# H3 and S5 sequence layers on one core: the halo rows of k are loaded unshifted and moved by one partition on TensorE, and the first loads change queues

## The chip, the core and the metric

The kernel runs on one core of a Trainium2 chip. The core has TensorE (PE, matrix products into PSUM), VectorE (DVE), ScalarE (ACT), GpSimd (POOL) and SyncE (SP); here SP only issues DMAs, and POOL issues some too. The metric is the device time of one execution in microseconds (us), lower is better.

## What is computed

Two layers with 2048 positions and 1024 channels stand side by side in the output. Layer A is an H3 layer: k is filtered over four neighbouring positions, multiplied by v, convolved with a long filter through an FFT of length 4096, and multiplied by q. Layer B is an S5 layer: a complex diagonal recurrence between two matrix products. Cut to what matters:

```python
# A: shift convolution with 4 taps, gate by v, long convolution, skip term, gate by q
k_pad = jnp.pad(k, ((0, 0), (3, 0), (0, 0)))
for t in range(4):
    k_shift = k_shift + k_pad[:, t:t + S, :] * shift_k[:, 3 - t][None, None, :]
kv = k_shift * v
y  = irfft(rfft(kv, 2 * S) * rfft(ssm_k, 2 * S))[:S]
a  = q * (y + kv * ssm_D)
# B: h[t] = Lam_bar * h[t-1] + Bu[t]
Bu = einsum("bld,pd->blp", x, B_bar)          # B_bar from Lambda, log_dt, B_re, B_im
y  = 2 * einsum("blp,dp->bld", hseq, C).real + x * Dskip
out = concat([a, b], axis=-1)                  # bfloat16
```

## The kernel before

**An order written out by hand.** The whole kernel is a list of tasks in a string, `ORDER` (L63 to L132). A word such as `wbe.6` calls the function `E["wbe"](6)`; `@S`, `@G` and `@D` choose SP, GpSimd or DVE for it; `:b9` and `:p0` name the SBUF or PSUM slots that it takes. Each engine runs its own instructions strictly in this order, so the place of a word decides what is queued behind it. DMAs go to SP by `spd` and to GpSimd by `gpd` unless the word says otherwise (L156, L157).

**The shift convolution of A (DVE).** Position 16n+s of k lies in partition n, row s. The tile `kring` holds 8 rows per partition; `kp.r` (L546) loads rows 2r and 2r+1 into slots (2r+4) mod 8. Position 16n needs the three positions before it, which lie in partition n-1. For them `kp.-2` and `kp.-1` load rows 12 to 15 into slots 0 to 3, one partition further down: partitions 1 to 127 take what belongs to 0 to 126, in two DMAs each (112 and 15 partitions). Partition 0 has no predecessor; a GpSimd memset (L370) fills its four slots with zeros. `kvm.r` (L561) multiplies the ring by the taps, `kva`, `kvb` and `kvc` add the products up and multiply by v.

**The taps.** `ld_w` (L376) loads `shift_k` as two rows into one partition; `wb.b` (L389) spreads 512 of its elements over all partitions by a matmul with a row of ones, and `wbe.b` (L394) copies the result from PSUM into `wbc`, all eight times. `kvm.0` needs all eight and the halo.

**The parameters of B.** `ld_par` (L237) loads four vectors into the 32 rows of `praw`; `par_T` transposes them on PE, `p32` copies them out on DVE, and `exp1`, `dve2`, `dve3`, `sm_pre`, `tabA1`, `exp2`, `sin0`, `tabA2`, `sin1`, `par_rest` and `sin2` make the constants and rotation tables from them on ACT and DVE.

**The matrix B.** `bl.j.w` loads a 128x1024 block of B_re or B_im, `bT.j.w` transposes it on PE (8 transposes into the PSUM slot p0 or p1), `bc.j.w` copies it into `BT` (L456). `bx` and `x` (L460, L466) are loads that transpose on the way, always on SP. `U.i.jp.jl` (L477) multiplies `BT` by x, `ue` evacuates, and `r1`, `r2`, `sc`, `r3`, `r4` run the recurrence on DVE.

**The transforms of A.** `hl` loads the long filter (`hk`), `hT` transposes it, `hc` evacuates on ACT, `am` and `hm` are the first DFT stage, `ae` and `he` evacuate it, `ast` and `hst` store it to DRAM for the later stages (L596 to L703).

Of the kernel before, what the change touches and what calls it, by code (L numbers as in the profile page):

```python
# [15 lines left out]
F32 = mybir.dt.float32  # L16
BF16 = mybir.dt.bfloat16
# [5 lines left out]
NR = 16  # L23
# [37 lines left out]
NX = 0  # L61

ORDER = """  # L63
bl.0.1:b0 bl.1.0:b11 bl.1.1@G:b14 ld_w@S:a0a11 bl.2.0@G:b13 ld_par bl.3.1@G:b12 bT.0.1:p0 bl.3.0:b10 bT.1.0:p1 kp.-2 kp.-1 bc.0.1 kp.0 ld_F@S par_T:p0
ld_sd@S:w0 p32 x.1:b9 bc.1.0@D wb.2:p0 exp1 wb.6:p1 wbe.6 dve2 wbe.2 dve3 wb.4:p1 sm_pre bl.0.0:b8 wb.3:p0 bx.5.1 wbe.4 wbe.3 wb.5:p1 tabA1:a10a9a8a7 wb.1:p0
wbe.1 wbe.5 bT.3.0:p0 exp2 tabA2 sin0 rt@G bT.3.1:p1 bx.7.0 sin1 par_rest kp.1 bc.3.1 bl.2.1:b7 x.0:b6 bc.3.0 wb.7:p1 wbe.7 bT.2.0:p0 vp.0:a5 wb.0:p1
bx.4.1 wbe.0 sin2 bT.0.0:p1 kvm.0:m0 bc.2.0 eo.1 bT.1.1:p0 hl.0:c0 eo.3 bx.7.1 bc.0.0 kva.0 bc.1.1 vp.2:a2 U.1.0.0:p1 bx.6.0 eo.0 bT.2.1:p0 eo.2 stt.1 U.1.0.1
bc.2.1 kvb.0:a6 z1 U.1.1.0:p0 stt.0 U.1.1.1 kvc.0 kvm.2:m0 am.0.1:d0 ue.1.1:a3 ue.1.0 hT.0.0:p0 kp.2 hT.0.3:p1 x.2:b0 hc.0.0:b5 ae.0.1:b4 hT.0.2:p0 am.1.0:d2
hc.0.2:b3 hm.0.0.0:d1 vp.1:a11 am.0.0:d0 ae.1.0:b2 bx.6.1 stt.3 he.0.0.0:b1 am.1.1:d2 kva.2 hT.0.1:p0 hc.0.3:b11 hm.0.0.1:d1 kp.3 hT.0.5:p1 bx.5.0 hc.0.5:b10
# [65 lines left out]
def full_kernel(ctx, tc, A_q, A_k, A_v, A_shift_k, A_ssm_k, A_ssm_D, B_x, B_Lre, B_Lim, B_Bre, B_Bim,  # L135
# [3 lines left out]
    nc = tc.nc  # L139
    P = 128  # L140
    S, D = A_q.shape[-2], A_q.shape[-1]
# [10 lines left out]
    q, k, v, x = A_q[0], A_k[0], A_v[0], B_x[0]  # L152
# [3 lines left out]
    spd = lambda o_, i_: (nc.gpsimd if on[0] == "G" else nc.sync).dma_start(o_, i_)  # L156
    gpd = lambda o_, i_: (nc.sync if on[0] == "S" else nc.gpsimd).dma_start(o_, i_)  # L157

    const = ctx.enter_context(tc.tile_pool(name="const", bufs=1))
# [3 lines left out]

    ident = const.tile([P, P], BF16, name="ident")
    make_identity(nc, ident[:])
    ones = const.tile([1, P], BF16, name="ones")
    nc.vector.memset(ones[:], 1.0)
    hpi = const.tile([P, 1], F32, name="hpi")
# [19 lines left out]
    kr = k.rearrange("(n s) d -> n s d", s=NR)  # L188
# [12 lines left out]
    st, pools, cms = {}, {}, {}  # L201

    def ap_pool(name):
        if name not in pools:
            for o in list(cms):
                cms.pop(o).__exit__(None, None, None)
            cms[name] = tc.tile_pool(name=name, bufs=1)
            pools[name] = cms[name].__enter__()
        return pools[name]
# [6 lines left out]
    def dtile(name):  # L216
        return psum.tile([P, 2, 512], F32, name=name, tag="pd%d" % cur["d"].pop(0), bufs=1)
# [12 lines left out]
    E = {}  # L230
# [135 lines left out]
    def kv_space():  # L366
        a1 = ap_pool("a1")
        st["wbc"] = a1.tile([P, 4, DV], BF16, name="wbc", bufs=1)
        st["kring"] = a1.tile([P, c["kr"], D], BF16, name="kring", bufs=1)
        nc.gpsimd.memset(st["kring"][0:1, 0:4, :].bitcast(F32), 0.0)  # L370
        if NX:
            st["kT"] = a1.tile([P, NX, NR + 4, P], BF16, name="kT", bufs=1)
            st["dg"] = a1.tile([P, NX, 4, P], BF16, name="dg", bufs=1)
# [74 lines left out]
    def copy(o_, i_):  # L448
        if on[0] == "D":
            nc.vector.tensor_copy(o_, i_)  # L450
        elif on[0] == "G":
            nc.gpsimd.tensor_copy(o_, i_)
        else:
            nc.scalar.copy(o_, i_)
# [90 lines left out]

    def kp(r):  # L546
        s0 = (2 * r + 4) % c["kr"]
        t_ = st["kring"][:, s0:s0 + 2, :]
        if r >= 0:
            spd(t_, kr[:, 2 * r:2 * r + 2, :])  # L550
        else:
            spd(t_[1:113, :, :], kr[0:112, NR + 2 * r:NR + 2 * r + 2, :])
            spd(t_[113:P, :, :], kr[112:P - 1, NR + 2 * r:NR + 2 * r + 2, :])
    E["kp"] = kp

    def vp(r):
        st["v", r] = k4("v", [P, 2, D])
        spd(st["v", r][:], vr[:, 2 * r:2 * r + 2, :])
# [197 lines left out]
@with_exitstack  # L756
def kernel(
    ctx: ExitStack,
    tc: tile.TileContext,
    A_q: bass.AP,  # L760
    A_k: bass.AP,
    A_v: bass.AP,
    A_shift_k: bass.AP,
    A_ssm_k: bass.AP,
    A_ssm_D: bass.AP,
    B_x: bass.AP,
    B_Lambda_re: bass.AP,
    B_Lambda_im: bass.AP,
    B_B_re: bass.AP,
    B_B_im: bass.AP,  # L770
    B_C_re: bass.AP,
    B_C_im: bass.AP,
    B_log_dt: bass.AP,
    B_Dskip: bass.AP,
    out: bass.AP,
):
    full_kernel(ctx, tc, A_q, A_k, A_v, A_shift_k, A_ssm_k, A_ssm_D, B_x, B_Lambda_re, B_Lambda_im,
                B_B_re, B_B_im, B_C_re, B_C_im, B_log_dt, B_Dskip, out)
# [30 lines left out]
```

## Time and profile before

| What | Value |
|---|---|
| median of 3 runs | 364.98 us (364.03 to 365.0) |
| profiled execution, its own time | 366.88 us |
| its span | 365.1 us, so 1.8 us lie around the span |
| granted TensorE clock, mean | 0.993 |
| first slices of 10 us, DMA share | 0.70, then 1.10, 1.25, 1.00 |
| POOL busy in the first 10 us | 4.51 us |

Times of the trace count from the start of the span. In a timeline, a row gives start, duration, engine, line, operation, output and input, and in brackets how long the engine sat idle before it and what ended that. "SPq" and "POOLq" are the queues' issue of DMAs. In a table by windows the columns are the stretch, its length, then busy time and instruction count of PE, PEld, DVE, ACT and POOL, the granted clock, the share of time that the DMA engines were busy, and GB/s.

### The profile page before, as it was taken

To read this page: it belongs to the slowest core of one execution; us is meant where nothing else is said; L and a number is where in the kernel's file an instruction comes from. 1 tells how busy PE (TensorE), PEld (TensorE's weight loads), DVE (VectorE), ACT (ScalarE), POOL (GpSimd) and SP (SyncE) were. 2 spreads that over 40 slices of the span, in tenths; PEclk is the share of its full clock that TensorE was granted. 3 is DMA by queue.
4 is the path that set the end of the run, shared out by engine and by line. 5 is a ranking of instruction groups with operands and counts; after the bars stand their busy time and mean duration, and the time that the engine had idled before them with its cause. 6 is when DMAs were issued, how large, how long until landed. Compare 5 with 4: busy or idle time off the path is not lost.

```text
span 365.1 us, 9551 instructions
## 1 busy us (share of the span) xinstructions
PE 336.0 (92%) x4109; PEld 215.8 (59%) x4109; DVE 319.3 (87%) x257; ACT 258.7 (71%) x330; POOL 65.4 (18%) x119
## 2 busy tenths in 40 slices
PE   4568898776999999999999999999999999999994
PEld 2366686664776986446475665654467568574441
DVE  3899999999999999999298999998998969989820
ACT  4799979558888976436477888887888784173641
POOL 4100111002014011300022313011041221344230
PEclk9999999998999999999999999999999999999999
DMA  6999998999998999888049977799986776989883
GB/s 205 275 333 308 251 406 307 213 343 248 265 287 281 204 225 307 263 228 203 0 111 303 212 275 233 235 227 355 282 239 226 203 257 193 348 254 316 293 246 116
DMA packets 74525, 91.95 MB, mean 252 GB/s; under 512 B 46369, under 2 KB 52401, under 8 KB 74482
## 3 DMA queue, kind: packets, MB, share of 16 engines
q1 hardware_dynamic: 64754, 58.55, 60.0%
q0 software_dynamic: 9728, 32.79, 27.1%
q8 instruction: 32, 0.52, 0.6%
q14 instruction: 11, 0.09, 0.1%
HBM read 47.28 MB, written 33.55 MB: 221 GB/s over the span
## 4 chain that ended last, share of the span: by engine, by line
PE 79%; ACT 7%; SPq 6%; DMA 5%; issue 2%; ACTq 0%
PE ps_y L532 31%; PE ps_u L477 28%; PE ps_a L664 5%; PE ps_a L694 4%; PE ps_a L630 3%; PE ps_a L596 3%; SPq L468 2%; DMA hk<-in_A_ssm_k_dram 2%; PE ps_a L725 2%; ACT ysb L601 2%; PE ps_y L537 2%; SPq L460 2%; ACT hT L622 2%; ACT ysbh L637 2%; DMA Ys_h<-ysbh 2%
## 5 line engine op out<-in xcount | busy, mean ns | idle before, releaser
L477 PEld LDWEIGHTS <-BT 128*128 128x128 bf16 x2048 | 119.5, 99 | 25.0 <-issue 13.2
L477 PE MATMUL ps_u<-xT,BT 128*128 128x128 bf16 x2048 | 126.8, 221 | 7.3 <-DMA xT<-in_B_x_dram 2.5
L532 PE MATMUL ps_y<-ct,h 128*128 128x512 bf16 x512 | 124.8, 380 | 0.0
L532 PEld LDWEIGHTS <-h 128*128 128x128 bf16 x512 | 44.3, 98 | 54.1 <-issue 12.5
L509 DVE TENSOR_TENSOR_SCAN h<-rtab,h 128x1040 bf16<-128x1040 f32 x32 | 72.5, 2307 | 0.1
L672 ACT CAST s<-ps_a 128x1024 bf16<-128x1024 f32 x64 | 62.0, 1016 | 12.7 <-PE ps_a L664 10.9
L542 ACT CAST yo<-ps_y 128x512 bf16<-128x512 f32 x32 | 18.9, 592 | 39.9 <-PE ps_y L532 32.6
L482 ACT CAST u<-ps_u 128x512 bf16<-128x512 f32 x64 | 37.9, 599 | 12.7 <-PE ps_u L477 12.6
L637 ACT CAST ysbh<-ps_a 128x1024 bf16<-128x1024 f32 x32 | 32.1, 1033 | 9.8 <-PE ps_a L630 8.4
L491 DVE TENSOR_TENSOR mt<-u,Z 128x4096 bf16<-128x4096 bf16 x16 | 36.6, 2285 | 2.8 <-ACT u L482 2.3
L569 DVE TENSOR_TENSOR mt<-kring,wbc 128x2048 bf16<-128x2048 bf16 (+3 forms) x14 | 35.7, 2588 | 1.6 <-DMA BT<-in_B_B_re_dram 1.6
L491 DVE TENSOR_TENSOR mt<-h,Z 128x4096 bf16<-128x4096 bf16 x16 | 36.6, 2289 | 0.2
L701 ACT CAST vsb<-ps_a 128x1024 bf16<-128x1024 f32 x32 | 30.9, 1015 | 7.2 <-PE ps_a L694 6.0
L601 ACT CAST ysb<-ps_a 128x1024 bf16<-128x1024 f32 x32 | 32.2, 1032 | 5.2 <-PE ps_y L537 1.5
L678 DVE TENSOR_TENSOR pq<-s,s 128x2048 bf16<-128x2048 bf16 x16 | 19.5, 1220 | 14.6 <-ACT s L672 14.4
L537 PE MATMUL ps_y<-Dd,xT 128*128 128x128 bf16 x128 | 28.0, 219 | 0.0
L157 POOL DMA_DIRECT2D Ys_kv<-ysb x14 | 7.8, 558 | 75.9 <-ACT ysb L601 75.9
L630 PE MATMUL ps_a<-hT,F1t 128*128 128x512 bf16 x64 | 19.3, 386 | 2.2 <-ACT hT L622 1.7
L596 PE MATMUL ps_a<-acc,F1t 128*128 128x512 bf16 x64 | 18.7, 384 | 2.3 <-ACT ysb L601 1.6
L682 DVE TENSOR_TENSOR s<-s,s 128x2048 bf16<-128x2048 bf16 x16 | 19.6, 1223 | 0.6
L503 DVE TENSOR_TENSOR h<-mt 128x2048 bf16<-128x2048 bf16 x16 | 19.6, 1224 | 0.4
L537 PEld LDWEIGHTS <-xT 128*128 128x128 bf16 x128 | 12.5, 98 | 12.3
(113 smaller groups left out, 326.6 us busy)
## 6 DMA issues: line engine op xcount, KB each, us to landing
Ys_h<-ysbh SPq DMA_DIRECT2D x23, 256.0 KB, 4.0
vv<-Vs POOLq DMA_DIRECT2D x11, 512.0 KB, 5.9
Ys_kv<-ysb SPq DMA_DIRECT2D x18, 256.0 KB, 4.2
Vs<-vsb SPq DMA_DIRECT2D x18, 256.0 KB, 3.5
kring<-in_A_k_dram SPq DMA_DIRECT2D x8, 512.0 KB, 4.3
v<-in_A_v_dram SPq DMA_DIRECT2D x8, 512.0 KB, 5.3
hk<-in_A_ssm_k_dram SPq DMA_DIRECT2D x8, 512.0 KB, 4.4
l2h<-Ys_h SPq DMA_DIRECT2D x8, 512.0 KB, 4.3
```

The source lines that it names most:

```text
L477: nc.tensor.matmul(pu[:, w, jl, :], BT[:, 2 * jp + jl, w, d, :], xT[:, d, :], start=(d == 0), stop=(d == ND - 1))
L482: nc.scalar.copy(u[:, :, 2 * jp:2 * jp + 2, :], st["pu", i, jp][:])
L491: nc.vector.tensor_mul(m, s_, w_)
L509: nc.vector.tensor_tensor_scan(gf, rtab[:].rearrange("p j t -> p (j t)"), gf, 0.0, ALU.mult, ALU.add)
L532: nc.tensor.matmul(py[:], h[:, 1 - w, j, 2:TP], st["CT", dh][:, j, w, :], start=(j == 0 and w == 0), stop=(j == NJ - 1 and w == 1))
L537: nc.tensor.matmul(py[:, dl * P:(dl + 1) * P], st["xT", i][:, d, :], Dd[:, d, :], start=False, stop=False)
L569: nc.vector.tensor_mul(m[:, :, j0:j0 + n, :], a_, wbc[:, j0:j0 + n, :].unsqueeze(1).to_broadcast([P, 2, n, DV]))
L601: nc.scalar.copy(st["ysb", r, u][:], st["pa", r, u][:].rearrange("p e d -> p (e d)"))
L630: nc.tensor.matmul(pd[:, e, :], F1t[:, u, :], st["hT", f, rp][:, e, :], start=True, stop=not sk)
L637: nc.scalar.copy(st["yh", f, rp, u][:], st["pa", f, rp, u][:])
L672: nc.scalar.copy(s16[:, u, :, :], st["ps", key, gq][u][:])
L701: nc.scalar.copy(vsb[:, gi, :].rearrange("p (e d) -> p e d", e=2), st["ps", "v", gq][gi][:])
```

## The change

The halo is loaded as it lies in DRAM, over all 128 partitions: row 13 into ring slot 0 and rows 14 and 15 into slots 6 and 7 (`kh`). A matrix `shf`, the identity with its columns moved by one, then moves each of the three rows by one partition on TensorE (`ksm`, two matmuls each of 512 columns), which leaves zeros in partition 0; three copies (`kse`, two on DVE, one on ACT) put the results from PSUM into slots 1 to 3. The memset of the ring goes. `kp` loses its case for negative r.

In the order, `ld_par` and `ld_w` move from SP to GpSimd's queue, and the three loads of B that were on GpSimd's queue move to SP, with `bl.3.0` behind them. `ksm` stands behind `wb.1`, `kse.0` behind it on DVE, and `kse.1` (ACT) and `kse.2` (DVE) behind `wbe.5`, ahead of `exp2` and `tabA2`.

```diff
 ORDER = """
-bl.0.1:b0 bl.1.0:b11 bl.1.1@G:b14 ld_w@S:a0a11 bl.2.0@G:b13 ld_par bl.3.1@G:b12 bT.0.1:p0 bl.3.0:b10 bT.1.0:p1 kp.-2 kp.-1 bc.0.1 kp.0 ld_F@S par_T:p0
-ld_sd@S:w0 ... sm_pre bl.0.0:b8 wb.3:p0 bx.5.1 wbe.4 wbe.3 wb.5:p1 tabA1:a10a9a8a7 wb.1:p0
-wbe.1 wbe.5 bT.3.0:p0 exp2 tabA2 sin0 rt@G bT.3.1:p1 bx.7.0 sin1 par_rest kp.1 ...
+bl.0.1:b0 bl.1.0:b11 ld_par@G ld_w:a0a11 bl.1.1:b14 bl.2.0:b13 bl.3.1:b12 bl.3.0:b10 bT.0.1:p0 bT.1.0:p1 bc.0.1 kh kp.0 ld_F@S par_T:p0
+ld_sd@S:w0 ... sm_pre bl.0.0:b8 wb.3:p0 bx.5.1 wbe.4 wbe.3 wb.5:p1 tabA1:a10a9a8a7 wb.1:p0 ksm.0:d0 ksm.1:d1 ksm.2:d2 kse.0@D
+wbe.1 wbe.5 kse.1 kse.2@D bT.3.0:p0 exp2 tabA2 sin0 rt@G bT.3.1:p1 bx.7.0 sin1 par_rest kp.1 ...
...
     make_identity(nc, ident[:])
+    shf = const.tile([P, P], BF16, name="shf")
+    nc.vector.memset(shf[:, 0:1], 0.0)
+    nc.vector.tensor_copy(shf[:, 1:P], ident[:, 0:P - 1])
...
-        nc.gpsimd.memset(st["kring"][0:1, 0:4, :].bitcast(F32), 0.0)
...
     def kp(r):
         s0 = (2 * r + 4) % c["kr"]
-        t_ = st["kring"][:, s0:s0 + 2, :]
-        if r >= 0:
-            spd(t_, kr[:, 2 * r:2 * r + 2, :])
-        else:
-            spd(t_[1:113, :, :], kr[0:112, NR + 2 * r:NR + 2 * r + 2, :])
-            spd(t_[113:P, :, :], kr[112:P - 1, NR + 2 * r:NR + 2 * r + 2, :])
+        spd(st["kring"][:, s0:s0 + 2, :], kr[:, 2 * r:2 * r + 2, :])
     E["kp"] = kp
+
+    raw = (0, 6, 7)
+
+    def kh():
+        spd(st["kring"][:, 0:1, :], kr[:, NR - 3:NR - 2, :])
+        spd(st["kring"][:, 6:8, :], kr[:, NR - 2:NR, :])
+    E["kh"] = kh
+
+    def ksm(j):
+        st["pk", j] = dtile("ps_a")
+        for e in range(2):
+            nc.tensor.matmul(st["pk", j][:, e, :], shf[:], st["kring"][:, raw[j], e * 512:(e + 1) * 512], start=True, stop=True)
+    E["ksm"] = ksm
+    E["kse"] = lambda j: copy(st["kring"][:, 1 + j, :], st["pk", j][:].rearrange("p e d -> p (e d)"))
```

More of the change, by code (lines that the diff above doesn't have):

```diff
@@ L63 @@
 ORDER = """
-bl.0.1:b0 bl.1.0:b11 bl.1.1@G:b14 ld_w@S:a0a11 bl.2.0@G:b13 ld_par bl.3.1@G:b12 bT.0.1:p0 bl.3.0:b10 bT.1.0:p1 kp.-2 kp.-1 bc.0.1 kp.0 ld_F@S par_T:p0
-ld_sd@S:w0 p32 x.1:b9 bc.1.0@D wb.2:p0 exp1 wb.6:p1 wbe.6 dve2 wbe.2 dve3 wb.4:p1 sm_pre bl.0.0:b8 wb.3:p0 bx.5.1 wbe.4 wbe.3 wb.5:p1 tabA1:a10a9a8a7 wb.1:p0
-wbe.1 wbe.5 bT.3.0:p0 exp2 tabA2 sin0 rt@G bT.3.1:p1 bx.7.0 sin1 par_rest kp.1 bc.3.1 bl.2.1:b7 x.0:b6 bc.3.0 wb.7:p1 wbe.7 bT.2.0:p0 vp.0:a5 wb.0:p1
+bl.0.1:b0 bl.1.0:b11 ld_par@G ld_w:a0a11 bl.1.1:b14 bl.2.0:b13 bl.3.1:b12 bl.3.0:b10 bT.0.1:p0 bT.1.0:p1 bc.0.1 kh kp.0 ld_F@S par_T:p0
+ld_sd@S:w0 p32 x.1:b9 bc.1.0@D wb.2:p0 exp1 wb.6:p1 wbe.6 dve2 wbe.2 dve3 wb.4:p1 sm_pre bl.0.0:b8 wb.3:p0 bx.5.1 wbe.4 wbe.3 wb.5:p1 tabA1:a10a9a8a7 wb.1:p0 ksm.0:d0 ksm.1:d1 ksm.2:d2 kse.0@D
+wbe.1 wbe.5 kse.1 kse.2@D bT.3.0:p0 exp2 tabA2 sin0 rt@G bT.3.1:p1 bx.7.0 sin1 par_rest kp.1 bc.3.1 bl.2.1:b7 x.0:b6 bc.3.0 wb.7:p1 wbe.7 bT.2.0:p0 vp.0:a5 wb.0:p1
 bx.4.1 wbe.0 sin2 bT.0.0:p1 kvm.0:m0 bc.2.0 eo.1 bT.1.1:p0 hl.0:c0 eo.3 bx.7.1 bc.0.0 kva.0 bc.1.1 vp.2:a2 U.1.0.0:p1 bx.6.0 eo.0 bT.2.1:p0 eo.2 stt.1 U.1.0.1
```

## The prediction

> **What bounds the kernel now.** I read the page first, then the busy times by windows of 10 us, then the timelines of PE and ACT, and last the chain of waits.
>
> ```profile
> PE 336.0 (92%) x4109; PEld 215.8 (59%) x4109; DVE 319.3 (87%) x257; ACT 258.7 (71%) x330; POOL 65.4 (18%) x119
> 20.00:30.00 10.00, 7.69 (x81) 7.42 (x81) 9.97 (x13) 10.00 (x23) 0.00 (x0) 1.00 1.25 339
> 110.00:120.00 10.00, 10.00 (x104) 7.02 (x103) 9.93 (x6) 8.86 (x12) 3.21 (x6) 1.00 0.84 278
> 350.00:360.00 10.00, 10.00 (x55) 4.70 (x53) 1.98 (x3) 3.10 (x4) 1.05 (x2) 1.00 0.75 220
> 106.82 0.59 PE L596 MATMUL ps_a<-acc,F1t 128*128 128x512 bf16 x2 [0.33 <-ACT ysbh L637]
> ```
>
> PE has the most work, and its last idle time ends at 106.82 us. From there to the end PE is busy in every window, and the chain of waits consists of PE pieces alone. The end is therefore the moment at which PE reaches that point, plus a fixed 258 us. The change touches only the first 31 us, so the question is by how much it moves what PE gets before 106.82.
>
> In the stretch 20 to 30 ACT has no gap at all (10.00 of 10), and DVE nearly none. Here is ACT from 10 us on, with PE beside it where it matters:
>
> ```profile
> 9.28 1.07 PE L391 MATMUL ps_a<-hk,ones 1*128 1x512 bf16 x2 [0.19 <-ACT wbc L454]
> 10.38 1.07 ACT L454 CAST wbc<-ps_a 128x512 bf16<-128x512 f32 x2 [0.67 <-PE ps_a L391]
> 11.35 0.22 ACT L262 ACTIVATE r<-a__163 128x8 f32<-128x8 f32 x1
> 14.05 1.90 ACT L454 COPY BT<-ps_t 128x1024 bf16<-128x1024 bf16 x2
> 17.59 0.59 ACT L454 CAST wbc<-ps_a 128x512 bf16<-128x512 f32 x1 [1.14 <-PE ps_a L391]
> 30.16 1.07 ACT L482 CAST u<-ps_u 128x512 bf16<-128x512 f32 x2
> 31.97 1.01 ACT L622 COPY hT<-ps_t 128x1024 bf16<-128x1024 bf16 x1 [0.73 <-PE ps_t L617]
> 32.88 1.02 ACT L601 CAST ysb<-ps_a 128x1024 bf16<-128x1024 f32 x1
> ```
>
> From `wbe.1` at 10.38 ACT works back to back through `exp2` (11.35), a table load, the sines and `bc.3.1`, `bc.3.0` (14.05). Its one wait, 1.14 us before `wbe.0` (17.59), is for PE work that itself waits for `bc.3.0`, so it moves along. From 17.59 ACT is full until `ue.1.0` ends at 31.23. Then it waits 0.73 us for the first filter transposes.
>
> ```profile
> 23.22 8.33 DMA hk<-in_A_ssm_k_dram
> 31.59 0.35 PE ps_t L617 x2
> 31.97 1.01 ACT hT L622
> ```
>
> That is the chain of waits in this place. It comes by the SP queue and the load of `hk`, and goes on by ACT, later by PE and ACT in turn. ACT's own queue reaches the same point 0.73 us earlier. So two paths run side by side, and ACT's has 0.73 us of slack.
>
> **The change, part by part.**
>
> *The added evacuation on ACT.* `kse.1` stands between `wbe.5` and `exp2`, in the middle of the unbroken run. It has the shape of the row at 32.88: 1.02 us. It must also wait for `ksm.1` on PE. `wb.1` ends at 10.35 (9.28 + 1.07); `ksm.0` and `ksm.1` are four matmuls of 512 columns. How long these take there the trace doesn't show, so I bound it by two groups, the first PE's at this time, the second from 30 us:
>
> ```profile
> L391 PE MATMUL ps_a<-hk,ones 1*128 1x512 bf16 x8 | 4.5, 586 | 3.3 <-ACT BT L454 2.0 <-ACT wbc L454 0.9 <-DVE dsk L253 0.3
> 29.96 0.59 PE L596 MATMUL ps_a<-acc,F1t 128*128 128x512 bf16 x2
> ```
>
> The early pair takes 1.07 with 0.59 for one, so about 0.48 from start to start; the late pair 0.59 with 0.38, so 0.21. With the early rate the fourth matmul ends at about 10.26 + 3 x 0.48 + 0.59 = 12.3; with the late rate at 11.4. `kse.1` then ends at 13.3 or 12.4, and `exp2` starts so much later than 11.35: 1.9 or 1.0 us. I take 1.9, since the early rows stand directly beside. The Trainium skill, "TensorE: Matmul & The Clock Gate", section "What's actually happening", says the array runs at half rate until it was busy for a window of about 3.4 us; the doubled spacing agrees, though the profile shows a granted clock of 1.00 in these stretches. By its full rate the term would be 1.0.
>
> *The tiny loads on GpSimd's queue.*
>
> ```profile
> 1.41 1.79 POOL L370 MEMSET kring<- 1x2048 f32 x1
> 3.16 0.69 POOL L156 DMA_DIRECT2D ld<-in_B_B_im_dram  x1
> 3.84 0.55 POOL L156 DMA_DIRECT2D ld<-in_B_B_re_dram  x1
> 5.62 0.18 PE L246 MATMUL ps_t<-ident,praw 32*128 32x32 bf16 x1 [0.25 <-ACT BT L454]
> 6.15 1.21 PE L391 MATMUL ps_a<-hk,ones 1*128 1x512 bf16 x2 [0.35 <-DVE dsk L253]
> Gt<-a_c_G POOLq DMA_DIRECT2D x1, 16.0 KB, 2.4
> ld<-in_B_B_re_dram POOLq DMA_DIRECT2D x1, 256.0 KB, 5.8
> ```
>
> Without the memset POOL issues from 1.41: one DMA at 0.69 and five at 0.55. The fourth of `praw` starts at 3.2, those of `ld_w` at 3.75 and 4.3. The small load `Gt` landed 2.4 after its issue, so `praw` lands at 5.6 and the taps at 6.15 and 6.7. Today `par_T` runs at 5.62 when its PSUM slot comes free, and the first taps are used at 6.15. That is on time to within 0.1. At the landing of a large load, 5.8, `praw` would come at 9.0, 3.4 late. Bounds 0 and 3.4; the size is that of `Gt`, so I take 0.1. In the Trainium skill, "DMA: Bandwidth & Descriptors", section "Specifications", GpSimd's path needs about 1 us to the first byte against 0.6 on SyncE's, which speaks against this move; by that the term would be 0.4 more on equal issue times. No row here splits the two.
>
> *The loads of B on SP, and the halo.*
>
> ```profile
> 1.20 0.42 SPq L156 DMA_DIRECT2D ld<-in_B_B_re_dram  x1
> 4.06 2.46 SPq L156 DMA_DIRECT2D kring<-in_A_k_dram  x5
> 7.57 3.13 SPq L468 DMA_TRANSPOSE xT<-in_B_x_dram  x1
> 4.00:5.00 1.00, 1.00 (x12) 1.00 (x11) 0.00 (x0) 0.45 (x1) 1.00 (x4) 1.00 0.56 110
> 16.25 0.58 SPq L156 DMA_DIRECT2D kring<-in_A_k_dram  x1
> ```
>
> SP issues sixteen DMAs before `x.1` at 7.57; after the change eleven. Two are out by 1.66; four blocks of B at 0.42 and five others at 0.49 (the row at 4.06) bring it there at about 5.8, some 1.7 us earlier. The DMA engines, at 0.56 in the fifth microsecond, get work without a gap, and the halo is 768 KB in place of 1016 KB (0.8 us at the 300 GB/s around). So `hk` lands 1.5 to 2.5 us earlier. But this earns only what waits for it. PE's and ACT's waits up to 31 us are for one another; the late loads of B are transposed behind `wb.1`, after 10.35. What goes is the wait for `hk`:
>
> ```profile
> 30.80 0.53 PE L617 MATMUL ps_t<-ident,hk 128*128 128x128 bf16 x6 [0.24 <-ACT u L482]
> 31.59 0.84 PE L617 MATMUL ps_t<-ident,hk 128*128 128x128 bf16 x10 [0.26 <-DMA hk<-in_A_ssm_k_dram]
> 33.03 0.66 PE L617 MATMUL ps_t<-ident,hk 128*128 128x128 bf16 x8 [0.59 <-ACT hT L622]
> ```
>
> Eight transposes take 0.66, so without the wait `hT.0.0` would end at 31.46 instead of 31.95: 0.5 us won (bounds 0 and 0.73, all of ACT's wait). What is late next is ACT itself, whose `ue.1.1` frees the slot. `kh` itself has 1.5 MB ahead of it. With 2.4 us to the first landing (`Gt`) and 280 to 340 GB/s (the quoted windows) its 0.75 MB are there at 9.0 to 10.4 (an estimate), in time for `ksm.1` at 11.2. `kp.1` overwrites slots 6 and 7, so SP must now wait for `ksm` there; that ends by 13 and `kp.1` issues at 16.25 today, so it costs nothing.
>
> *The copies on DVE.*
>
> ```profile
> 6.01 0.68 DVE L450 COPY BT<-ps_t 128x1024 bf16<-128x1024 bf16 x1
> 13.34 1.23 DVE L302 SCALAR_TENSOR_TENSOR tab<-tab 128x1024 f32<-128x1024 f32 x1
> 18.27 4.42 DVE L569 TENSOR_TENSOR mt<-kring,wbc 128x8192 bf16<-128x8192 bf16 x1 [1.55 <-DMA BT<-in_B_B_re_dram]
> 28.17 1.22 DVE L590 TENSOR_TENSOR acc<-acc,v 128x2048 bf16<-128x2048 bf16 x1
> ```
>
> `kse.0` and `kse.2` cost 0.68 to 1.23 each; I take 1.2, so 2.4 in all, ahead of `tabA2`. DVE now waits 1.55 before `kvm.0` at 18.27. (The row names a DMA that `kvm.0` doesn't read; `wbe.0` ended at 18.18.) With `wbe.0` 2.0 later the cover is 3.5, so the copies are hidden. If ACT were not later, 0.9 would show. `kvc.0` ends 2.0 later, at 31.4; `am.0.1` behind it on PE, today at 29.96, follows the `U` products, which are equally late by ACT's copies. The two instructions that make `shf` (128 columns) come before `p32`, and DVE has nothing else to do until `par_T` at 5.62: nothing.
>
> *Sum.* 1.9 + 0.1 on ACT, less 0.5 of the wait for `hk`: `hc.0.0` comes 1.5 us later, and I find nothing between 32 and 106.82 that gives it back, as PE and ACT release each other there. The profiled execution would go from 366.88 (span 365.1) to 368.4; it lies 1.9 above the median of the runs, 364.98, so the median should be **366.5 us**.
>
> **The rivals.** About 0.3%, or 1.1 us, is what a measurement of this kernel tells from no change.
>
> *The shift runs at PE's late rate.* The matmuls follow `wb.5` and `wb.1` without a gap, which speaks for it; that the row at 6.15 and the one at 9.28 have the same slow rate speaks against. Then 1.0 + 0.1 - 0.5 = +0.6: 365.6, no change. Later slack that takes up a microsecond of the 1.5 ends in the same place.
>
> *The head start of the DMAs carries on (not slower).* The place is `x.3`:
>
> ```profile
> 61.74 2.62 SPq L468 DMA_TRANSPOSE xT<-in_B_x_dram  x1
> 68.22 1.07 PE L477 MATMUL ps_u<-xT,BT 128*128 128x128 bf16 x16 [2.52 <-DMA xT<-in_B_x_dram]
> ```
>
> If the queues stay 2.5 us ahead, this wait goes: +1.5 - 2.5 = -1.0, and with the late rate of PE -1.9: 363.1 to 364.0. It decides once the transposed load of `x.3` is issued more than 1.5 us sooner. Against it: SP issues that load at 61.74, in the order behind a store (`hst.0.3.1`) that waits for ACT.
>
> *The tiny loads come late.* In a busy queue `praw` lands like a large load: +3.4 more, 369.9; a third of that 367.6. For: the engines are now full from 2.5 us on. Against: the loads are a few packets.
>
> *The change doesn't do what it says.* If the loads of B on SP hold `kh` back past 11.2, `ksm` waits, and each microsecond is one on ACT; this is a variant of the former.
>
> **How the numbers follow.** Forecast (+1.1 to +2.2) 0.38; late rate or slack (-1.1 to +1.1) 0.33; head start (below -1.1) 0.16; late loads (above +2.2) 0.13. So slower has 0.51, within 0.3% 0.33, faster 0.16. The range of 8 in 10 leaves out the ends of both outer cases: 363.4 to 368.6. The forecast's own is 366.1 to 367.2.
>
> **What would show it.** `exp2` on ACT at about 13.3 (right), at 12.4 (PE fast) or at 11.4 (the sum is wrong from the start). `par_T` at 5.6 to 5.8, or far behind. `x.1` on SP near 5.9. `hc.0.0` at 33.5 with no DMA in its wait. PE's last idle end at 108.3 in place of 106.82. The prediction is wrong if ACT has idle time between 17 and 31 that I don't see, or if the waits between 55 and 107 turn out to hang on DMAs and not on ACT.

## The result, and the profile after

| | before | after |
|---|---|---|
| median of the runs, us | 364.99 (364.03 to 367.47, 4 runs) | 369.5 (368.76 to 371.05, 4 runs) |
| ratio, 95% interval | | 1.0135 (1.009 to 1.018) |
| profiled execution, us (span) | 366.88 (365.1) | 370.0 (368.2) |

The change makes the kernel 4.5 us slower. The forecast of 366.5 had the sign right and a third of the size; 369.5 lies outside its range, 363.4 to 368.6. A later set of runs (e13) gave 1.0171 (1.012 to 1.0221). Ratios leave out single executions far above the others of their kernel: 574.67 in e2, 1873.38 in e4, 373.63 in e8, and 368.14 of before in the runs beside e13 to e15.

The page's row of busy times and three windows of the changed kernel come first:

```profile
PE 331.9 (90%) x4069; PEld 215.5 (59%) x4115; DVE 321.2 (87%) x261; ACT 259.7 (71%) x331; POOL 65.0 (18%) x121
```

```profile
20.00:30.00 10.00, 5.79 (x46) 4.69 (x46) 8.30 (x16) 8.85 (x20) 0.00 (x0) 0.50 1.26 316
110.00:120.00 10.00, 9.95 (x97) 6.75 (x97) 9.81 (x7) 9.54 (x12) 4.73 (x8) 1.00 0.94 318
350.00:360.00 10.00, 9.84 (x60) 4.63 (x59) 1.99 (x3) 4.04 (x5) 2.63 (x6) 1.00 0.85 242
```

From 110 us on PE is full, as in before, so the end is still PE's last idle end plus some 258 us. (PE's busy time lacks 46 matmuls against its 4115 weight loads, so its fall from 336.0 means nothing.) What differs lies ahead of 30 us: from 20 to 30 PE has 5.79 us of work where it had 7.69, and ACT, full before, has 1.15 us of gaps. (That gap is no new one: it is the wait before `wbe.0`, 1.14 us at 17.59 in before, which now falls into this stretch.)

The next view is PE's timeline of the changed kernel (start, duration, instruction, count, and in brackets the idle time before it with what ended it):

```profile
8.39 0.18 PE L249 MATMUL ps_t<-ident,praw 32*128 32x32 bf16 x1 [2.94 <-DMA praw<-in_B_Dskip_dram]
9.00 1.22 PE L393 MATMUL ps_a<-hk,ones 1*128 1x512 bf16 x2 [0.42 <-DVE dsk L256]
12.15 1.07 PE L393 MATMUL ps_a<-hk,ones 1*128 1x512 bf16 x2 [0.19 <-ACT wbc L456]
13.15 2.74 PE L563 MATMUL ps_a<-kring,shf 128*128 128x512 bf16 x6
35.46 1.16 PE L628 MATMUL ps_t<-ident,hk 128*128 128x128 bf16 x16 [0.46 <-ACT u L484]
109.55 0.59 PE L607 MATMUL ps_a<-acc,F1t 128*128 128x512 bf16 x2 [0.33 <-ACT ysbh L648]
```

`par_T`, the first row, stood at 5.62 in before and waited for ACT. Now it waits 2.94 us for the last row of `praw`, and comes 2.77 later. The shift (six matmuls of 512 columns) follows `wb.1` without a gap. The transposes of `hk` wait for ACT and no longer for a DMA. The last idle time ends at 109.55, which is 2.73 later than before's 106.82.

ACT's timeline of the same kernel, at the places that correspond to 11.35 and 31.97 of before:

```profile
15.07 1.01 ACT L456 CAST kring<-ps_a 128x1024 bf16<-128x1024 f32 x1 [0.74 <-PE ps_a L563]
15.98 0.21 ACT L265 ACTIVATE r<-a__163 128x8 f32<-128x8 f32 x1
36.16 1.01 ACT L633 COPY hT<-ps_t 128x1024 bf16<-128x1024 bf16 x1 [0.26 <-PE ps_t L628]
```

`exp2` is 4.63 later: 2.77 from `par_T`, and 1.86 that arise between the two, nearly all of it by the wait of `kse.1` for PE (0.74) and its copy (1.01). `hc.0.0` is 4.19 later, 0.44 less, since the wait for `hk` is gone. So 2.77 + 1.86 - 0.44 = 4.19.

Why `praw` is late begins in the timeline of POOL's issues and the groups of DMA issues (queue, count, size, median us from issue to landing):

```profile
1.52 0.67 POOL L156 DMA_DIRECT2D praw<-in_B_log_dt_dram  x1
3.21 0.52 POOL L156 DMA_DIRECT2D praw<-in_B_Dskip_dram  x1
```

```profile
hk<-in_A_shift_k_dram POOLq DMA_DIRECT2D x2, 4.0 KB, 5.2
praw<-in_B_log_dt_dram POOLq DMA_DIRECT2D x1, 2.0 KB, 3.8
praw<-in_B_Dskip_dram POOLq DMA_DIRECT2D x1, 2.0 KB, 5.0
```

The issues come where the prediction put them, the fourth at 3.21. But 2 KB need 3.8 to 5.0 us to land. Beside them the windows of the changed kernel (the last two columns are the busy share of the DMA engines and GB/s):

```profile
4.00:5.00 1.00, 1.00 (x12) 0.95 (x11) 0.00 (x0) 0.37 (x1) 0.90 (x4) 1.00 1.00 294
5.00:6.00 1.00, 0.45 (x5) 0.18 (x2) 0.00 (x0) 0.65 (x1) 0.00 (x0) 1.00 0.98 321
```

In the same microsecond before, the share was 0.56 (its row stands in the prediction). The engines now have a backlog of large blocks while the small loads are under way. Whether the backlog delays them, or GpSimd's queue, is what the experiments ask first.

### The profile page after: what moved, and what is told of

Its sections match the earlier page's. It is cut to its first block, busy times and chain, and to the rows that moved or that the text cites. A ratio compares the mean times of both kernels' runs of the same rounds, so it can differ in the third digit from the quotient of the medians.

```text
span 368.2 us, 9520 instructions
## 1 busy us (share of the span) xinstructions
PE 331.9 (90%) x4069; PEld 215.5 (59%) x4115; DVE 321.2 (87%) x261; ACT 259.7 (71%) x331; POOL 65.0 (18%) x121
## 4 chain that ended last, share of the span: by engine, by line
PE 70%; ACT 11%; DMA 7%; DVE 4%; issue 3%; SPq 3%; POOL 1%; ACTq 0%; POOLq 0%; DVEq 0%
PE ps_y L534 28%; PE ps_u L479 23%; PE ps_a L675 4%; PE ps_a L705 4%; PE ps_y L539 2%; PE ps_a L736 2%; DMA Ys_h<-ysbh 2%; PE ps_a L641 2%; DMA l2k<-Ys_kv 2%; ACT ysb L612 2%; ACT ysbh L648 2%; ACT BT L456 1%; DMA Ys_kv<-ysb 1%; DMA praw<-in_B_Dskip_dram 1%; PE ps_a L607 1%
## 5 line engine op out<-in xcount | busy, mean ns | idle before, releaser
L534 PE MATMUL ps_y<-ct,h 128*128 128x512 bf16 x483 | 119.6, 379 | 1.3 <-issue 0.6
L505 DVE TENSOR_TENSOR h<-mt 128x2048 bf16<-128x2048 bf16 x16 | 19.6, 1224 | 0.4
L523 DVE TENSOR_TENSOR h<-mt 128x2048 bf16<-128x2048 bf16 x16 | 19.4, 1216 | 0.3
L641 PE MATMUL ps_a<-hT,F1t 128*128 128x512 bf16 x55 | 16.6, 379 | 3.2 <-ACT hT L633 1.7
```

Of the source, the lines that this page charges most:

```text
L534: nc.tensor.matmul(py[:], h[:, 1 - w, j, 2:TP], st["CT", dh][:, j, w, :], start=(j == 0 and w == 0), stop=(j == NJ - 1 and w == 1))
L641: nc.tensor.matmul(pd[:, e, :], F1t[:, u, :], st["hT", f, rp][:, e, :], start=True, stop=not sk)
```

## The experiments

Two theories stand against each other. **Backlog:** small loads are late when they are issued into full DMA engines, by whatever queue; in before the memset held POOL's large loads back until 3.16 and so kept the engines free. **Queue:** GpSimd's queue itself is slow. A second question is how much of each delay reaches the end.

The table has the stations by which the runs are compared: the start of `par_T`, `exp2` and `hc.0.0` and the end of PE's last idle time in each profiled execution, in us, with that execution's time, and the ratio of the timed runs to before where there were several.

| kernel | `par_T` | `exp2` | `hc.0.0` | last idle end | time | ratio, 95% interval |
|---|---|---|---|---|---|---|
| before | 5.62 | 11.35 | 31.97 | 106.82 | 366.88 | |
| before, again (e5) | 5.72 | 11.45 | 31.93 | 105.23 | 365.37 | |
| after | 8.39 | 15.98 | 36.16 | 109.55 | 370.0 | 1.0135 (1.009 to 1.018) |
| after, again (e10) | 8.14 | 16.56 | 36.70 | 109.33 | 369.61 | |
| after, again (e13) | 7.86 | 15.87 | 36.01 | 111.24 | 372.28 | 1.0171 (1.012 to 1.0221) |
| e1 small loads on SP | 5.57 | 13.61 | 33.75 | 105.32 | 365.41 | 1.0098 (1.0058 to 1.0138) |
| e1 again (e11) | 5.53 | 13.23 | 33.37 | 105.07 | 365.2 | |
| e1 again (e14) | 5.56 | 14.31 | 34.45 | 109.55 | 370.87 | 1.0113 (1.0062 to 1.0164) |
| e2 halo alone | 8.04 | 15.53 | 35.67 | 108.31 | 368.36 | 1.0073 (1.0044 to 1.0103) |
| e3 small loads on ACT | 6.44 | 13.93 | 34.12 | 107.00 | 367.1 | 1.0041 (1.0005 to 1.0078) |
| e4 queues alone | 9.61 | 15.84 | 35.99 | 107.58 | 367.87 | 1.0089 (1.0054 to 1.0124) |
| e6 memset late | 7.53 | 13.26 | 33.39 | 105.08 | 365.11 | 1.0023 (0.9989 to 1.0057) |
| e7 after, `kse.1` in a gap | 8.04 | 14.66 | 34.62 | 108.69 | 369.13 | 1.0117 (1.0074 to 1.016) |
| e8 = e1 + e7 | 5.59 | 11.31 | 31.73 | 103.80 | 363.9 | 1.0044 (1.0004 to 1.0084) |
| e8 again (e12) | 5.59 | 11.32 | 32.80 | 104.27 | 364.57 | |
| e8 again (e15) | 5.62 | 11.35 | 31.63 | 104.50 | 364.84 | 1.0042 (1.001 to 1.0073) |
| e9 small loads in quiet | 6.38 | 15.16 | 35.30 | 108.47 | 368.75 | |

### Why the small loads are late: e1, e2, e3, e4, e6, e9

**e1**, the changed kernel with the small loads back on SP, ahead of the blocks of B:

```diff
-bl.0.1:b0 bl.1.0:b11 ld_par@G ld_w:a0a11 bl.1.1:b14 ...
+bl.0.1:b0 bl.1.0:b11 ld_w@S:a0a11 ld_par bl.1.1:b14 ...
```

> The changed kernel with one thing undone: the four loads of ld_par and the two of ld_w go back to SP's queue, where they stood before (behind the first two blocks of B); the loads of B stay on SP, the halo stays on TensorE. My theory: the loss is two terms, 2.8 us because praw lands late, and 1.9 us for the copy kse.1 on ACT, less 0.5 us that the wait for hk gave back. Then par_T starts at 5.6 us again instead of 8.39, hc.0.0 at 33.4 instead of 36.16, and the time falls by 2 to 3 us against the changed kernel, to about 366.5 to 367.5. Rival: the blocks of B on SP are what holds things up, and the tiny loads only show it; then par_T moves little and the time stays near 369.5.

`par_T` is back at 5.57, so the 2.8 us come from where the small loads are issued; queue and place in the order changed together here. `exp2` is 2.26 later than in before: SP now has twelve issues ahead of `kh` where after has six, PE waits 0.39 for `kring` within the shift, and `kse.1` waits 1.29 for PE. The runs miss the expectation: their median is 368.17, and by the ratio some 3.6 us over before.

**e2**, the halo on TensorE with the queues of before, POOL's three blocks included:

```diff
-bl.0.1:b0 bl.1.0:b11 ld_par@G ld_w:a0a11 bl.1.1:b14 bl.2.0:b13 bl.3.1:b12 bl.3.0:b10 bT.0.1:p0 bT.1.0:p1 bc.0.1 kh ...
+bl.0.1:b0 bl.1.0:b11 bl.1.1@G:b14 ld_w@S:a0a11 bl.2.0@G:b13 ld_par bl.3.1@G:b12 bT.0.1:p0 bl.3.0:b10 bT.1.0:p1 kh bc.0.1 ...
```

> The halo on TensorE alone: the first loads stand on the queues of the kernel before, the memset is gone. My theory: par_T at 5.6 us, exp2 at 13.2 (1.9 later than before), hc.0.0 at about 33.4; the time 1 to 2 us over before, like the run with the tiny loads back on SP. Rival (the queues of B matter by themselves): this run is more than 0.7 us better or worse than that one.

The expectation missed, and this miss says most. PE's timeline and POOL's in e2:

```profile
8.04 0.18 PE L249 MATMUL ps_t<-ident,praw 32*128 32x32 bf16 x1 [2.60 <-DMA praw<-in_B_Dskip_dram]
```

```profile
1.50 0.69 POOL L156 DMA_DIRECT2D ld<-in_B_B_im_dram  x1
2.19 0.55 POOL L156 DMA_DIRECT2D ld<-in_B_B_re_dram  x1
```

The small loads are on SP's queue, as in before, and `praw` is as late as in after. What differs from before is that the memset is gone, so POOL's blocks go out at 1.50 in place of 3.16. **e6** is the cross-check, before with nothing but the memset moved behind POOL's three loads:

```diff
-bl.3.1@G:b12 bT.0.1:p0 ...
+bl.3.1@G:b12 kz bT.0.1:p0 ...
-        nc.gpsimd.memset(st["kring"][0:1, 0:4, :].bitcast(F32), 0.0)
+    E["kz"] = lambda: nc.gpsimd.memset(st["kring"][0:1, 0:4, :].bitcast(F32), 0.0)
```

> The kernel before with one move: GpSimd's memset stands behind its three loads of B instead of ahead of them. Theory 'backlog': the memset had held these loads back until the tiny loads were through; without it the blocks fill the DMA engines from 2.5 us on, par_T slips from 5.6 to about 8 us as in the run with the halo alone, and the time rises by 1.5 to 2.5 us. Rival: the tiny loads are late by something else in the changed kernels (the halo's own loads); then par_T stays at 5.6 and the time at that of before.

```profile
7.53 0.18 PE L246 MATMUL ps_t<-ident,praw 32*128 32x32 bf16 x1 [2.07 <-DMA praw<-in_B_Dskip_dram]
```

That row of PE's timeline shows `par_T` 1.91 late, by the memset's place alone. `hc.0.0` keeps 1.42 of it; of the 1.5 to 2.5 us expected in the time nothing is shown, since the ratio, 1.0023 with 1 inside its interval, doesn't tell this from no change. **e4** is the other half of the change, its queues with before's halo and the memset behind the small loads:

```diff
-bl.0.1:b0 bl.1.0:b11 bl.1.1@G:b14 ld_w@S:a0a11 bl.2.0@G:b13 ld_par bl.3.1@G:b12 bT.0.1:p0 bl.3.0:b10 ...
+bl.0.1:b0 bl.1.0:b11 ld_par@G ld_w:a0a11 kz bl.1.1:b14 bl.2.0:b13 bl.3.1:b12 bl.3.0:b10 bT.0.1:p0 ...
```

> The queues alone: tiny loads on GpSimd, the blocks of B on SP, the halo by the shifted loads as before, the memset behind the tiny loads on GpSimd. My theory: par_T at 8.4 us, no added copy on ACT, so hc.0.0 at 31.97 + 2.8 - 0.5 = 34.3 and the time 2 to 3 us over before. Rival (the head start of the DMAs is worth something once the copy is gone): less than 1.5 us over before.

It has `par_T` latest of all, at 9.61 in place of the expected 8.4, with landings up to 6.8 us, although its engines were busy to 0.66 and 0.92 only in the fifth and sixth microsecond. The repeat of after, e10, is alike: 0.62 and 0.86, and landings of 3.7 to 5.6. So the share alone doesn't tell how late a small load is; what adds to it in e4 was not separated. **e9** then keeps GpSimd's queue and takes the backlog away: SP loads the last part of `praw` a second time behind its first two blocks, which makes it wait before it issues more.

```diff
-... ld_w:a0a11 bl.1.1:b14 ...
+... ld_w:a0a11 ld_q bl.1.1:b14 ...
+    E["ld_q"] = lambda: spd(st["praw"][3 * NJ:4 * NJ, :], B_Dskip.rearrange("(j i) -> j i", i=P))
```

> After with one more small load: SP loads the last row group of praw a second time, behind its first two blocks of B, and so waits for GpSimd's load of praw before it issues the other blocks. The small loads stay on GpSimd's queue, in a machine that has only two blocks (512 KB) in flight. If the backlog of blocks made them late (my theory): the loads of praw land 2.0 to 2.8 us after their issue in place of 3.8 to 5.0, and par_T runs at 5.6 to 6.3. If GpSimd's path is slow by itself: landings 3.8 to 5.0 us again, par_T at 8 or later. The end says little here, since the blocks come some 2 us later: 366 to 371 us.

First the groups of DMA issues of e9, then its windows:

```profile
hk<-in_A_shift_k_dram POOLq DMA_DIRECT2D x2, 4.0 KB, 1.8
praw<-in_B_log_dt_dram POOLq DMA_DIRECT2D x1, 2.0 KB, 2.8
praw<-in_B_Dskip_dram POOLq DMA_DIRECT2D x1, 2.0 KB, 1.7
```

```profile
3.00:4.00 1.00, 0.47 (x5) 0.48 (x6) 0.00 (x0) 0.00 (x0) 1.00 (x3) 1.00 0.69 248
4.00:5.00 1.00, 1.00 (x13) 1.00 (x11) 0.00 (x0) 0.40 (x1) 0.90 (x4) 1.00 0.03 4
```

The same instructions at the same times (the fourth again at 3.21) on the same queue land in 1.7 us in place of 5.0, once the engines are at 0.03 and not at 1.00. `par_T` runs at 6.38, just past the upper end of what was expected, since SP's second load of those rows, issued at 4.93, must land too. The time is 368.75, with all blocks behind it late. The large blocks are shown to be what makes the small loads late, and GpSimd's queue by itself is not. **e3**, the small loads issued by ACT (`ld_par@A ld_w@A`, with ACT as a third issuer in `spd` and `gpd`), adds a price of that place:

> The changed kernel with the six tiny loads issued on ACT's queue in place of GpSimd's; SP as in the changed kernel. Theory 'backlog' (the tiny packets share DMA engines that SP's blocks keep full from 2.5 us on): the loads land late here too, 3.5 us or more after their issue, only the issue is earlier. Theory 'GpSimd's path': they land within 2.4 us, par_T at 5.6 us, and the time is that of the run with the tiny loads on SP, 366.5 to 367.5.

`par_T`, at 6.44, waits there for ACT, whose six issues come ahead of its first table load and copies. PE takes the last row of `praw` in as weights at 5.31, so it landed at most 3.3 us after its issue at 2.03. That is sooner than the 3.5 expected by "backlog"; whether it is within the 2.4 of the other theory, this bound doesn't tell. Only three blocks were out by 2.03, so this run doesn't separate the queue from the moment of issue.

What does put the runs in order is how many blocks of B had been issued when the last row of `praw` was. In after the sixth is SP's issue at 3.08, ahead of the row's own at 3.21:

```profile
3.08 0.43 SPq L156 DMA_DIRECT2D ld<-in_B_B_re_dram  x1
```

With two blocks out (e1 and e9, and before with a third just being issued) the row landed within 2.0 us of its issue; with three (e3) within 3.3; with five (e2, e6) after about 4.7 and 4.2; with six (after and its repeats, e7, e4) after 4.5 to 6.3. These are single profiles, and the number was not varied by itself.

### What reaches the end: e7, e8 and the repeats

**e5**, the kernel before once more, asks which of its waits are its own:

> The kernel before, unchanged, for a second profile: the first one was 1.9 us over the median, and had a wait of 2.52 us for x.3 at 68 us. If that wait belongs to that execution alone, the second profile lacks it and PE's last idle time ends near 104 to 105; if it belongs to the kernel, it is there again and PE's last idle time ends at 106.8.

The wait of 2.52 us for `x.3` at 68.22, on which a rival of the prediction rested, isn't there: PE waits 1.63 at that place, for ACT. Of two executions, one has it. **e7** and **e8** move `kse.1` to ACT's gap ahead of `wbe.0`, e7 in the changed kernel and e8 in e1:

```diff
-wbe.1 wbe.5 kse.1 kse.2@D bT.3.0:p0 exp2 ... wb.7:p1 wbe.7 bT.2.0:p0 ...
+wbe.1 wbe.5 kse.2@D bT.3.0:p0 exp2 ... wb.7:p1 wbe.7 kse.1 bT.2.0:p0 ...
```

> The changed kernel with one move: kse.1 goes on ACT from ahead of exp2 to behind wbe.7, where ACT waits 1.15 us for PE. My theory: the 1.9 us of that term vanish: exp2 at 14.1 in place of 15.98, hc.0.0 at 34.3 in place of 36.16, the time 1 to 2 us under the changed kernel. Rival: ACT's run is not what sets hc.0.0 (another engine is as late), and the time stays within 0.7 us of 369.5.

> Both terms taken away: tiny loads on SP ahead of the blocks, kse.1 in ACT's gap; the halo on TensorE and the blocks of B on SP stay. My theory: par_T at 5.6, exp2 at 11.4, hc.0.0 at 31.5, the time within 0.5 us of the kernel before (364.2 in the last runs) or a little under it. Rival: something else of the change costs too; then it stays 1 us or more over before.

In e8 all early stations are those of before, so they are accounted for: the small loads and `kse.1`. The runs' median, 366.37, is still 1.4 us over before's 365.01, where at most 0.5 was expected. In e7 `hc.0.0` comes 1.54 sooner than in after, but the last idle end only 0.86, and the median of its runs, 369.73, is no lower than after's 369.5. PE's timeline shows where it went, first e7, then the same products in after, and behind them the windows of e7 (the third column from the right is the granted clock):

```profile
43.86 3.44 PE L479 MATMUL ps_u<-xT,BT 128*128 128x128 bf16 x32 [0.54 <-ACT hT L633]
45.40 1.95 PE L479 MATMUL ps_u<-xT,BT 128*128 128x128 bf16 x32 [0.54 <-ACT hT L633]
```

```profile
40.00:44.00 4.00, 2.11 (x22) 1.61 (x23) 3.97 (x4) 3.25 (x5) 0.00 (x0) 1.00 0.73 239
44.00:48.00 4.00, 4.00 (x40) 3.63 (x39) 4.00 (x4) 3.18 (x5) 1.15 (x3) 0.57 0.94 162
```

The 32 products take 1.95 in after and 3.44 in e7, at a granted clock of 0.57. In e7 PE was busy for 1.97 of the 3.86 us before them, but so it was in after, with the same waits; why one execution has the half rate and the other not stays open. The timed runs of e1 spread over 5 us while its profiled execution was as short as before. So the three main kernels were profiled again, and timed together on one chip:

> The changed kernel again, a second profile. If the early delay is a property of the kernel: par_T at 8.0 to 8.7, exp2 at 15.5 to 16.3, hc.0.0 at 35.7 to 36.5 and PE's last idle end 2.5 to 4.2 us behind 105.2 to 106.8, at 107.7 to 111. If the 2.8 us of par_T were a chance of one execution, par_T comes at 5.6 to 6.5 here.

> The small loads on SP as in before, the halo on TensorE: a second profile of a kernel whose runs spread from 365.4 to 370.5 us. Where the profiled execution is a long one (over 368): theory A, that PE falls to half rate for some microseconds between 32 and 50 (idle stretches of PE there, then matmuls of doubled spacing), shows PE's groups late by 1 to 2 us behind that stretch with hc.0.0 still at 33.5 to 34; theory B, that the early landings vary, shows par_T or exp2 later than 5.6 and 13.6 by the same amount. Where it is a short one (under 367.5), neither is seen.

> The small loads on SP and kse.1 moved into ACT's gap behind wbe.7, a second profile (runs so far 363.9 to 373.6 us, the profiled one 363.9 with PE's last idle end at 103.80). Early stations as in before again: exp2 at 11.3, hc.0.0 at 31.7. By theory A a long execution shows PE at half rate between 32 and 50 us and is late behind that stretch; by theory B it is late at par_T or exp2 already.

> The changed kernel, timed beside e14 and e15 on one chip. All theories: 368.8 to 371.0 us, 3.5 to 5.5 above the kernel before.

> The halo on TensorE with the small loads on SP (e1), timed again. If the added copy on ACT reaches the end as its 1.9 us at exp2 say: 1.5 to 2.5 us above the kernel before, 366.5 to 367.5. If the 3.3 of the first ten runs belong to the kernel: 368 again, with runs in two groups. If the two profiled executions (365.4 and 365.2) are the rule, so that later slack takes up the 1.9: within 0.7 of the kernel before.

> e1 with kse.1 behind wbe.7, timed again. Its early stations are those of the kernel before, so if they alone set the end, it takes as long as before (364.5 to 365.5). If the halo on TensorE costs something that these stations don't show: 366 or more, as in the first ten runs.

In all three profiles of after `par_T` is 2.2 to 2.8 late, so this belongs to the kernel. In e10 `exp2` and `hc.0.0` are 0.3 and 0.2 beyond what was expected: the taps, the last of the small loads, come late as well there (`wb.6` waits for them until 10.22). In e12 `exp2` is on time, but `hc.0.0`, at 32.80, is 1.1 later than expected: the raw rows of k land later, PE waits 0.57 and 0.23 for them, and ACT then waits 1.55 for PE.

e13 and e14 happened to profile long executions, e11 a short one of e14's kernel. ACT's and PE's timelines of e14, with a window:

```profile
77.96 1.01 ACT L633 COPY hT<-ps_t 128x1024 bf16<-128x1024 bf16 x1 [1.96 <-DMA Ys_kv<-ysb]
```

```profile
79.03 1.05 PE L479 MATMUL ps_u<-xT,BT 128*128 128x128 bf16 x16 [3.49 <-ACT hT L633]
80.50 3.43 PE L479 MATMUL ps_u<-xT,BT 128*128 128x128 bf16 x32
```

```profile
80.00:84.00 4.00, 4.00 (x38) 3.50 (x36) 3.97 (x2) 0.38 (x1) 0.00 (x0) 0.57 1.17 274
```

And the same two places in e11:

```profile
74.81 1.01 ACT L633 COPY hT<-ps_t 128x1024 bf16<-128x1024 bf16 x1 [0.65 <-DMA Ys_kv<-ysb]
```

```profile
75.88 1.05 PE L479 MATMUL ps_u<-xT,BT 128*128 128x128 bf16 x16 [1.42 <-ACT hT L633]
77.29 1.95 PE L479 MATMUL ps_u<-xT,BT 128*128 128x128 bf16 x32
```

A store of `ysb`, issued by SP behind a transposed load, must land before ACT gets its way. The chain of waits gives it here, e14 first:

```profile
67.45 2.59 SPq L470
...
70.09 7.80 DMA Ys_kv<-ysb
```

```profile
66.11 1.90 SPq L470
...
68.05 6.68 DMA Ys_kv<-ysb
```

In e14 the stations up to `hc.0.0` are 1.08 later than in e11, SP's transposed load takes 0.69 longer and the store 1.12 longer; PE waits 3.49 in place of 1.42 and then runs 32 products in 3.43 in place of 1.95, at a clock of 0.57. That is 1.08 + 2.07 + 1.48 = 4.63 against 4.48 at the last idle end. e13 has the same at 80.31 (a wait of 3.21). So the spread of the runs, as far as two long executions show it, is not theory A as put (half rate between 32 and 50), and theory B (early landings that vary) gives 1.08 of it in e14; the rest the chain of waits puts on a late store at 70 to 80 us, with PE's half rate behind it. In the profiles of before PE waits 1.61 and 1.10 at that place. Why the store is late in some executions, and whether the changed kernel brings this about more often, stays open.

By the medians of the runs that shared a chip, e15 is 0.9 above before (365.7 against 364.79, between its two expectations), e14 2.6 above e15 and again near e1's 368, and e13 2.7 above e14 (368.29 and 370.96). These are differences of medians whose intervals reach over about 1.8 us to each side. They fit 2.2 to 2.8 us of late small loads and 1.9 to 3.0 that `exp2` is late in e1, e11 and e14, which would then reach the end nearly whole. The earlier runs, each set against its own runs of before, split the loss otherwise: by their ratios after is only some 1.3 us above e1 and 0.7 above e7, and e1 2.0 above e8. So each part's share at the end is known to a microsecond or two only. The 0.9 of e15 (0.1 to 0.7% by its interval; 0.0 to 0.8% in e8) has no station in e8 or e15 that shows it; the late `hc.0.0` of e12 may be a part of it, which is not shown. None of the versions beats the kernel before.

## Why the prediction failed in its size

**The failed step is "the tiny loads on GpSimd's queue".** It was taken at 0.1 us from bounds of 0 and 3.4, and measured 2.77. The issue times were right. The landing was taken from `Gt`, 2.4 us, by the likeness of size, though `Gt`, issued at 115.74, was not loaded in engines that stayed full: in before their share is 0.95 from 115 to 116, 0.75 in the next microsecond and 0.18 in the one after. The rows that spoke against it were quoted in the prediction: the share of 0.56 in the fifth microsecond, and the memset that held POOL's loads until 3.16. The prediction used them as a gain for `hk` ("get work without a gap") and didn't ask what the small loads would meet in that full stretch. In the runs the landing goes with the blocks issued ahead of it (e2, e6, e9), and not with the size of the load. The rival "the tiny loads come late" had the place and the mechanism, with +3.4 and 369.9; its chance of 0.13 was too small. The prediction didn't see that the memset was the cover, so that also the halo alone (e2) brings the delay.

**The copy on ACT was right at its place:** 1.9 predicted, 1.86 measured between `par_T` and `exp2`; what it costs at the end, 2.6 by e14 less e15 and 2.0 by e1 less e8, is less certain. The six matmuls took 2.74, so 0.43 from start to start, near the early rate's 0.48 and twice the late rate's 0.21; the rival with PE's late rate falls. **The wait for `hk`** gave 0.44 of a predicted 0.5, and no DMA ends the wait any more. **The copies on DVE** took 1.22 each where 1.2 was taken, and stayed hidden.

**The order on SP:** `x.1` was issued at 6.73, not at 5.9 (before: 7.57). `kh` and `kp.0` took the time that was put down for them, but from one block of B to the next it is 0.47 where 0.42 was taken, and `ld_F` and `ld_sd` took 1.75 together where 0.98 was. Nothing waits for `x.1` there.

**"PE and ACT release each other" between 32 and 106.82** was too simple. Between 66 and 80 the chain of waits goes through SP's queue and a store in after, in e14, and in before's first profile too (e5's keeps to PE and ACT). The prediction named waits on DMAs in this stretch as a sign of being wrong, and they are there. The early delay still went through: over all profiles in the table, `hc.0.0` runs from 31.63 to 36.70 and the last idle end from 103.80 to 111.24, and from e12 to e10 3.90 at the one are 5.06 at the other. But a single execution is off by up to 2 to 4 us by what the store and PE's clock do, so before's own 106.82 was a poor base: in e5 it is 105.23.

**The head start of the DMAs** earned nothing that a run shows. The wait for `x.3` it was to remove is missing in before's second profile (e5).

## What to carry to other kernels

A small load on the critical path is to be costed by the large blocks that have been issued ahead of it and are still under way, on whatever queue, and not by its size. An instruction that looks idle, such as a memset ahead of large loads, can be what keeps those loads off the engines; before it goes, ask which transfers it held back and who overtakes whom. And a wait that one profile shows is taken as the kernel's own only when a second execution shows it.

## What the runs showed of the hardware

**Small loads in full engines.** 2 KB landed 5.0 us after issue in after, at a DMA share of 1.00, and 1.7 us in e9, at 0.03. The Trainium skill, "DMA: Bandwidth & Descriptors", section "Issuing engines are not separate DMA queues", says that transfers of all issuers end on the same 16 DMA engines and interleave there; e2, late on SP's queue through POOL's blocks, agrees. The same page of the Trainium skill, section "Queues, rings and completion order", says that an engine turns from one queue to the next after a packet, by which the few packets of a small load should pass quickly. In after they were alone on their queue, all blocks being on SP's, and needed 5.0 us. The packets themselves start late: between 3 and 4 us GpSimd's queue moved 2 of them in after and 92 in e9, with the same issues. No run here shows what they waited for inside the engine.

**PE's half rate.** 32 products took 1.95 us in after, but 3.43 after PE had waited 3.49 (e14), 2.50 a little after a wait of 3.21 (e13), and 3.44 in e7, each time with a granted clock of 0.57 in a window of 4 us that holds all or part of them. The Trainium skill, "TensorE: Matmul & The Clock Gate", section "What's actually happening", puts the array back to half rate after an idle window of about 3.4 us whose phase is free. The wait of 3.49 agrees; that of 3.21 in e13 is shorter than the window, and in e7 no wait in the 4 us before is over 1.10. The waits alone don't decide it either, since after has those of e7 and runs the products in 1.95. In these executions the half rate cost up to 1.5 us on top of the wait.
